# Two queues for the small exchanges of a spectral layer, another order of its partitions, and contiguous writes in one copy

## The chip, the cores and the metric

The kernel runs on one core of one Trainium2 chip. The metric is the device time of one execution in microseconds (us).

Names: PE is TensorE, ACT is ScalarE, DVE is VectorE, POOL is GpSimd, SP is SyncE. SPq is SyncE's own queue of instructions, PEld are PE's weight loads.

## The reference

Two layers, each a global spectral filter (2-D FFT of the normalised activations, a product with complex weights, inverse FFT) and a channel MLP, both with residuals. x is 2048 x 576 in bf16.

```python
def spectral(x, w_r, w_i):
    X = jnp.fft.rfft2(x.astype(jnp.float32), axes=(-2, -1)) * (w_r + 1j * w_i)
    return jnp.fft.irfft2(X, s=x.shape[-2:], axes=(-2, -1)).astype(jnp.bfloat16)
# mlp: gelu(layernorm(y) @ w1 + b1) @ w2 + b2 with 4608 hidden columns
for _ in range(2):
    x = x + spectral(layernorm(x), w_r, w_i)
    x = x + mlp(layernorm(x))
```

## The kernel before

The FFT over the 2048 rows is cut into 16 x 128. Between its two factors the data must change partitions, which no matmul here does: that is an *exchange*. Each of 16 tiles (128 partitions x 580 values of bf16, 145 KB) is written by one DMA into 8 partitions of a big array. A layer has two: exchange 1 brings y1 into v_sb, between the first DFT stage and the second (`dft_u`); exchange 2 brings h into b_sb, before the last inverse DFT (`idft_v`). Each consumer needs a slice of all tiles, so it starts when the last exchange has landed. PE meanwhile multiplies zeros (`keep_busy`).

```python
    # first stage, one tile: DFT over the columns, scaled by the layernorm's 1/std while it is copied out of PSUM
            z = work.tile([P, 2, KP], BF16, tag="z", bufs=3)
            nc.scalar.activation(
                out=z[:].rearrange("p r (j o) -> p r o j", o=2),     # writes every second element
                in_=pz[:, :, 0:KP].rearrange("p o (r j) -> p r o j", r=2),
                func=ACT.Copy, scale=self.st.pop(("rs", t)),
            )
    # ... dft_v makes y1 from z; then
            exchange(self.vx, t, y1)

    def exchange(dst, slot, src):
        p0 = 32 * (slot // 4) + slot % 4
        ins = nc.sync.dma_start(out=dst[p0 : p0 + 29 : 4], in_=src).ins   # 128 partitions -> 8
        # ... (declares that exchanges into other partitions don't wait for each other)

    # second stage
        keep_busy(12)                       # zeros while exchange 1 lands
        # dft_u, weigh, join, idft_c -> h, exchange(hx, E_ORDER[n], h)
    # last inverse stage
            for n in self.early[:2]:
                self.put_x(n)               # work that needs no exchange
            keep_busy(16)                   # zeros while exchange 2 lands
            self.idft_v(0)                  # first reader of exchange 2
```

Weights for the middle stage are loaded during the first stage by DMAs that GpSimd issues, paced by marks on earlier instructions. GpSimd issues in program order, so an issue that waits holds up those behind it.

## Time and profile before

747.18 us, the median of 6 runs (746.68 to 747.85); the profiled run has a span of 745.1 us.

| quantity of layer 0, us from the start of the span | before |
|---|---|
| first matmul that makes a y1 | 10.98 |
| last y1 copy ends | 37.80 |
| first matmul on v_sb (exchange 1 is in) | 41.63 |
| last h copy ends | 64.93 |
| first matmul on b_sb (exchange 2 is in) | 69.99 |

The first part of the page: each engine's busy time, its share of the span and its instructions.

```profile
PE 726.9 (98%) x5038; PEld 454.1 (61%) x5038; DVE 273.0 (37%) x932; ACT 314.3 (42%) x530; POOL 61.6 (8%) x114
```

PE at 98% does not mean that nothing can be won: the fillers count as busy. The view of waits says where PE still stood idle in the first 75 us. The columns are: who waited, on what, for how long in total, how often, the longest.

```profile
PE pss_156 L337 <- DVE xf L315: 2.0, 1, 2.0
PE psb_705 L496 <- DMA v_sb<-shared_113: 1.3, 1, 1.3
PE pss_1036 L567 <- DMA b_sb<-shared_691: 0.9, 1, 0.9
```

The second and third lines are what the change is after. The timeline around exchange 1 (start, duration, engine, line, operation; in brackets the idle time before it and what ended it):

```profile
37.09 0.40 ACT L399 CAST shared_113<-pss_680 128x290 bf16<-128x290 f32 x1 [0.94 <-PE pss_680 L398]
37.34 0.46 DVE L399 CAST shared_113<-pss_684 128x290 bf16<-128x290 f32 x1
37.54 2.77 PE L214 MATMUL pss_692<-zeros 128*128 128x512 bf16 x12 [0.24 <-ACT shared_113 L399]
38.17 0.61 SPq L481 DMA_DIRECT2D v_sb<-shared_113  x1
41.63 0.66 PE L496 MATMUL psb_705<-v_sb,c_f_83 128*128 128x290 bf16 x4 [1.32 <-DMA v_sb<-shared_113]
...
```

The last y1 is complete at 37.34 + 0.46 = 37.80. Its DMA is issued at 38.17, its data land at 41.39 (read from the semaphore's updates in the trace), and the reader starts at 41.63. These three pieces, 0.37 + 3.22 + 0.24 us, are the gap of 3.83 us. Layer 1's gap is 2.98. The same around exchange 2:

```profile
64.47 0.46 DVE L531 CAST shared_691<-psb_997 128x290 bf16<-128x290 f32 x1 [1.11 <-PE psb_997 L527]
...
64.49 0.67 PE L593 MATMUL psb_1009<-x_sb,halves 128*128 128x288 bf16 x4
...
65.48 3.65 PE L214 MATMUL pss_1019<-zeros 128*128 128x512 bf16 x16
...
69.99 0.60 PE L567 MATMUL pss_1036<-c_r_84,b_sb 128*128 128x256 bf16 x4 [0.87 <-DMA b_sb<-shared_691]
```

And one z copy of the first stage, in which ACT is busy nearly all the time; a plain copy of the same size takes 0.65 us.

```profile
23.65 0.94 ACT L423 ACTIVATE z<-psb_445,rs 128x580 bf16<-128x580 f32 x1
```

Busy times by stretches of 2 us, of PE, PEld, DVE, ACT and POOL, then the granted clock, the mean busy share of the 16 DMA engines and what they moved in GB/s (which is KB/us). The exchanges alone keep the share near one half:

```profile
14.00:16.00 2.00, 1.68 (x16) 1.03 (x13) 1.66 (x5) 2.00 (x5) 0.84 (x2) 1.00 0.85 208
...
32.00:34.00 2.00, 2.00 (x21) 1.59 (x19) 1.90 (x8) 1.72 (x5) 0.00 (x0) 1.00 0.57 191
34.00:36.00 2.00, 1.87 (x22) 1.53 (x21) 1.34 (x2) 1.54 (x3) 0.00 (x0) 1.00 0.53 178
```

### The profile page before, as it was taken

To read this page: it belongs to the slowest core of one execution; us is meant where nothing else is said; L and a number is where in the kernel's file an instruction comes from. 1 tells how busy PE (TensorE), PEld (TensorE's weight loads), DVE (VectorE), ACT (ScalarE), POOL (GpSimd) and SP (SyncE) were. 2 spreads that over 40 slices of the span, in tenths; PEclk is the share of its full clock that TensorE was granted. 3 is DMA by queue.
4 is the path that set the end of the run, shared out by engine and by line. 5 is a ranking of instruction groups with operands and counts; after the bars stand their busy time and mean duration, and the time that the engine had idled before them with its cause. 6 is when DMAs were issued, how large, how long until landed. Compare 5 with 4: busy or idle time off the path is not lost. (4 is left out here: it accounts for less than half of the span.)

```text
span 745.1 us, 12420 instructions
## 1 busy us (share of the span) xinstructions
PE 726.9 (98%) x5038; PEld 454.1 (61%) x5038; DVE 273.0 (37%) x932; ACT 314.3 (42%) x530; POOL 61.6 (8%) x114
## 2 busy tenths in 40 slices
PE   7989999999999999999999999999999999999998
PEld 4655744784488447844775575467547744774476
DVE  7975860366036603630364869001400140010011
ACT  7865865015521552155324777530362045105600
POOL 4120012001000100000004000020100010000000
PEclk9999999999999999999999999999999999999999
DMA  8744825311121112110028401460001010200000
GB/s 272 232 139 162 250 88 189 100 44 34 29 62 52 35 27 63 44 35 0 22 40 235 122 10 59 149 158 18 36 10 44 17 44 0 45 17 8 1 17 17
DMA packets 49417, 54.45 MB, mean 73 GB/s; under 512 B 29892, under 2 KB 41104, under 8 KB 49360
## 3 DMA queue, kind: packets, MB, share of 16 engines
q1 hardware_dynamic: 41328, 23.99, 12.5%
q0 software_dynamic: 7600, 29.10, 12.2%
q8 instruction: 39, 0.64, 0.3%
q10 hardware_dynamic: 432, 0.58, 0.2%
q14 instruction: 18, 0.15, 0.1%
HBM read 29.34 MB, written 8.59 MB: 51 GB/s over the span
## 5 line engine op out<-in xcount | busy, mean ns | idle before, releaser
L806 PEld LDWEIGHTS <-h_sb 128*128 128x128 bf16 x2304 | 224.9, 98 | 58.6 <-issue 1.0
L761 PEld LDWEIGHTS <-w_sb 128*128 128x128 bf16 x1152 | 109.4, 98 | 142.4 <-issue 17.2
L274 DVE BATCH_NORM_STATS2 stats<-x_sb 128x6 f32<-128x288 bf16 x110 | 43.8, 440 | 1.1 <-DMA x_sb<-in_A_x_dram 1.1
L720 DVE TENSOR_SCALAR xn<-x_sb,mv,rs 128x576 bf16<-128x576 bf16 x24 | 9.4, 426 | 66.7 <-DMA quad_1769<-xn 27.7
L769 PEld LDWEIGHTS <-w1r_sb 64*128 64x128 bf16 x288 | 10.8, 94 | 24.5 <-issue 17.0
L802 DVE TENSOR_TENSOR xb<-x_sb,b_bc 128x576 f32<-128x576 bf16 x32 | 23.9, 748 | 0.0
L723 POOL COPY xn<-xn 128x64 bf16<-128x64 bf16 x24 | 6.4, 267 | 155.2 <-DVE xn L720 155.2
L527 PEld LDWEIGHTS <-h_sb 128*128 128x128 bf16 x128 | 12.1, 97 | 11.6 <-issue 6.2
L496 PEld LDWEIGHTS <-c_f_83 128*128 128x128 bf16 x128 | 12.3, 97 | 8.8 <-issue 3.2
L775 ACT ACTIVATE h_sb<-psb_5993,b_sb 128x512 bf16<-128x512 f32 x2 | 1.3, 684 | 37.9 <-PE psb_5993 L769 37.9
L775 ACT ACTIVATE h_sb<-psb_7189,b_sb 128x512 bf16<-128x512 f32 x2 | 1.3, 684 | 37.8 <-PE psb_7189 L769 37.8
L775 ACT ACTIVATE h_sb<-psb_6591,b_sb 128x512 bf16<-128x512 f32 x2 | 1.3, 683 | 37.8 <-PE psb_6591 L769 37.8
L829 DVE TENSOR_TENSOR x_sb<-psb_7429,xb 128x576 bf16<-128x576 f32 x1 | 0.8, 757 | 43.4 <-PE psb_7429 L806 43.4
L829 DVE TENSOR_TENSOR x_sb<-psb_4049,xb 128x576 bf16<-128x576 f32 x1 | 0.8, 758 | 39.5 <-PE psb_4049 L806 39.5
L214 PEld LDWEIGHTS <-zeros 128*128 128x128 bf16 x95 | 9.4, 100 | 9.5 <-issue 1.7
L352 DVE TENSOR_TENSOR xf<-ef 128x256 bf16<-128x256 f32 (+1 forms) x56 | 13.6, 305 | 0.5
L829 DVE TENSOR_TENSOR x_sb<-psb_6233,xb 128x576 bf16<-128x576 f32 x1 | 0.8, 757 | 33.6 <-PE psb_6233 L806 33.6
L829 DVE TENSOR_TENSOR x_sb<-psb_6831,xb 128x576 bf16<-128x576 f32 x1 | 0.8, 758 | 33.6 <-PE psb_6831 L806 33.6
L435 PEld LDWEIGHTS <-c_k_82 128*128 128x128 bf16 x120 | 11.1, 98 | 2.4
L419 PEld LDWEIGHTS <-xT 128*128 128x128 bf16 x96 | 9.6, 101 | 3.9 <-issue 1.1
L829 DVE TENSOR_TENSOR x_sb<-psb_3245,xb 128x576 bf16<-128x576 f32 x1 | 0.8, 757 | 28.7 <-PE psb_3245 L806 28.7
L678 ACT ACTIVATE h_sb<-x_sb 128x576 bf16<-128x576 bf16 x16 | 11.2, 699 | 0.1
(1367 smaller groups left out, 1500.6 us busy)
## 6 DMA issues: line engine op xcount, KB each, us to landing
w_sb<-in_B_w_dram SPq DMA_DIRECT2D x16, 288.0 KB
v_sb<-in_B_w_dram POOLq DMA_DIRECT2D x4, 1152.0 KB, 5.9
h_sb<-const_i POOLq DMA_DIRECT2D x8, 384.0 KB, 6.6
shared_1465<-in_B_w_dram POOLq DMA_DIRECT2D x2, 1440.0 KB, 7.9
shared_5390<-in_B_w_dram POOLq DMA_DIRECT2D x2, 1440.0 KB, 7.5
v_sb<-shared_113 SPq DMA_DIRECT2D x16, 145.0 KB
b_sb<-shared_691 SPq DMA_DIRECT2D x16, 145.0 KB
v_sb<-shared_4645 SPq DMA_DIRECT2D x16, 145.0 KB
```

The source lines that it names most:

```text
L214: nc.tensor.matmul(pw[:], lhsT=zeros[:], rhs=zeros[:, 0:1].to_broadcast([P, 512]), start=True, stop=True)
L274: nc.vector.bn_stats(out=stats[:, h, :], in_=x_sb[:, t, h * DH : (h + 1) * DH])
L352: nc.vector.tensor_tensor(out=xf[:, at0 : at0 + 2 * n].rearrange("p (g d) -> p g d", g=2), in0=ef[:, :, first : first + n], in1=ef[:, :, b ...
L419: nc.tensor.matmul(pz[:, o, 0:KP], lhsT=xT[:, ci, :], rhs=c_fd[:, 3 * o + q, :], start=(q == 0), stop=(q == 2),)
L435: nc.tensor.matmul(py[:, r, 0:KP], lhsT=c_k1[:, pl, :], rhs=z[:, ri], start=(q == 0), stop=(q == 1))
L496: nc.tensor.matmul(px[:, o, 0:KP], lhsT=c_f2[:, e, pl, :], rhs=vx[:, e, ri, :], start=(q == 0), stop=(q == 1))
L527: nc.tensor.matmul((ph, odd)[o][:, o, 0:KP], lhsT=i1[:, n % 4, pl, :], rhs=xp[:, ri, :], start=(q == 0), stop=(q == 1))
L678: nc.scalar.activation(out=at(h_sb, [P, D], 512 * 34), in_=x_sb[:, self.quad[i], :], func=(ACT.Copy, ACT.Square)[k], accum_out=self.s12[:, ...
L761: nc.tensor.matmul(acc[p][q], lhsT=w1_sb[:, ci, fc * 128 : (fc + 1) * 128], rhs=yT[:, ci, :], start=(first and ci == 0), stop=(not first a ...
L769: nc.tensor.matmul(acc[p][q], lhsT=w1r_sb[rows, p, :], rhs=yT[rows, 4, :], start=first, stop=not first)
L802: nc.vector.tensor_tensor(out=xb[:], in0=xr, in1=b2_bc[:].rearrange("p (h n) -> p h n", h=2), op=ALU.add)
L806: nc.tensor.matmul(po[:, h, 0:DH], lhsT=hts[fc][:, i * 128 : (i + 1) * 128], rhs=w2_chunk(fc)[:, h * DH : (h + 1) * DH], start=(fc == 0), ...
```

## The change

The intent: (a) let ACT write z contiguously and read PSUM in steps instead; (b) spread layer 0's exchanges over two queues, so that they use more than eight DMA engines; (c) let successive tiles write to partitions of different halves.

```diff
-SLOT_ROWS = [8 * (4 * (p // 32) + p % 4) + (p // 4) % 8 for p in range(128)]
+SLOT_ROWS = [8 * (4 * (0, 2, 1, 3)[p // 32] + p % 4) + (p // 4) % 8 for p in range(128)]
@@ dft_d
-                out=z[:].rearrange("p r (j o) -> p r o j", o=2),
-                in_=pz[:, :, 0:KP].rearrange("p o (r j) -> p r o j", r=2),
+                out=z[:].rearrange("p r (j o) -> p r j o", o=2),
+                in_=pz[:, :, 0:KP].rearrange("p o (r j) -> p r j o", r=2),
@@ dft_v                      (room is None in layer 1)
-            exchange(self.vx, t, y1)
+            exchange(self.vx, t, y1, nc.gpsimd if self.room is not None and order.index(t) % 2 == 0 else nc.sync)
@@
-    def exchange(dst, slot, src):
-        p0 = 32 * (slot // 4) + slot % 4
-        ins = nc.sync.dma_start(out=dst[p0 : p0 + 29 : 4], in_=src).ins
+    def exchange(dst, slot, src, queue=nc.sync):
+        p0 = 64 * (slot // 4 % 2) + 32 * (slot // 8) + slot % 4
+        if queue is nc.gpsimd:
+            nc.gpsimd.nop()
+        ins = queue.dma_start(out=dst[p0 : p0 + 29 : 4], in_=src).ins
@@ idft_c                     (queues is 2 in layer 0, 1 in layer 1)
-            exchange(hx, E_ORDER[n], h)
+            exchange(hx, E_ORDER[n], h, nc.gpsimd if queues == 2 and n % 2 == 0 and n < NT - 2 else nc.sync)
```

Below, "tile 14" and "tile 15" are the last two in order of work.

More of the change, by code (lines that the diff above doesn't have):

```diff
@@ L485, in exchange, with middle @@
         before.append(ins)
-    def middle(vx, hx, wks, i1s, loads):
+    def middle(vx, hx, wks, i1s, loads, queues):
         st = {}
@@ L912 @@
             }
-        middle(vx, hx, wks, i1s, mid_loads)
+        middle(vx, hx, wks, i1s, mid_loads, 2 - li)
         if li == 0:
```

## The prediction

> **What bounds the kernel.** TensorE is busy 98% of 745.1 us (page, first part), mostly in the two MLPs, which the change leaves alone. But part of that is filler: matmuls on zeros while PE waits for exchanges. The change acts on the spectral stages of layer 0, the first 70 us. There (timeline) three things can give:
>
> 1. *Exchange 1.* The last y1 copy ends at 37.80 us, the filler at 40.31; the first matmul on v_sb starts at 41.63. The waits view gives PE 1.3 us for DMA v_sb<-shared. This gap is 3.83 us; layer 1's is 2.98.
> 2. *Exchange 2.* Last h copy 64.93; filler ends 69.13; first matmul 69.99: PE waits 0.9 us for b_sb. Layer 1 waits nothing here.
> 3. *The z copies.* From 10 to 36 us ScalarE is busy 93-100%, VectorE 84-99% (stretches of 2 us); a pair of tiles takes 3.60 or 3.84 us.
>
> **Why the exchanges are late.** From 30 to 41 us and 59 to 67 us only SyncE's queue moves data, at a DMA share flat at 0.53-0.54 and 175-180 KB/us: half of the 16 engines. The Trainium skill ("DMA: Bandwidth & Descriptors", on why a DMA increments its semaphore by 16) says that the engine count is the largest up to 16 dividing both slowest dimensions, here 128 and 8, and that SyncE takes the lowest; the trace agrees. Until 30 us weight loads share these engines and the exchange gets only about 35 KB/us, so a backlog builds: at 38.2 us (last issue) 2.6 exchanges are still to move. An exchange alone (layer 1) takes 1.3 us to its first packet and 1.2 us of packets.
>
> **What changes.** Half of layer 0's exchanges (8 of 16; 7 of 16 in the second) go to GpSimd. The same section says that its 8-engine copies go round by a cursor, so about half of these should land on the idle upper eight: engines 0-7 lose a quarter of 290 KB each, 3.3 us at 22 KB/us. No backlog should remain at the last issue. Added: GpSimd issues of 0.55-0.75 us each, on an engine 8% busy, in line with the loads, which have slack. I expect the first v_sb matmul 2.8 us after the last y1 (gain 1.0) and the first b_sb matmul right behind the filler (gain 0.8). The filler caps these at 1.3 and 0.9.
>
> **z** takes 0.92 us for 580 elements, a plain copy 0.65; at 290, 0.59 against 0.40. So about 0.11 us is fixed ("ScalarE: Activation LUTs", What ACT_TABLE_LOAD costs: 93 ns for a pointer operand) and 0.28 ns per element is the strided write. Contiguous writes save up to 0.16 us each, if reading PSUM alternately from two banks is free, which nothing in the trace shows. VectorE takes about 3.55 us a pair and then binds, so 14 copies save 0.8 us of stage, not 2.2. In layer 1 these copies hide under PE.
>
> **Sum:** 747.2 - 1.0 - 0.8 - 0.8 = 744.6 us; range 742.9 to 746.9. Faster by over 2%: 0.01; within 2%: 0.98; slower by over 2%: 0.01.
>
> **What would show it.** z mean about 0.77 us; last y1 near 37.0; DMA share above 0.54 within 30-38 us; gap from y1 to the first v_sb matmul about 2.8 us; no PE wait for b_sb in layer 0; layer 1 unchanged.
>
> **What would make it wrong.** The alternate PSUM read may cost more than the write saves: with z at 1.1 us ScalarE binds and the stage grows by 2 us, giving about 747. GpSimd's copies may all use the lower eight engines, or land late behind loads in the same rings; then the exchange gains vanish. Waits for exchanges in GpSimd's order might hold loads up.

## More of the kernel before

All runs told here were with a granted clock of 0.995 to 1.0.

In exchange 1, tile 14 goes to GpSimd and tile 15 to SyncE.

The filter's weights are tiny (0.05 x 0.02 in standard deviation): the comparison with the reference tolerates much in the spectral path.

## The result, and the profile after

The changed kernel takes 746.57 us, the median of 10 runs (745.92 to 747.90), against 747.49 us for the kernel before in the same rounds (746.51 to 749.60, 20 runs). The ratio is 0.9989, with a 95% interval from 0.9980 to 0.9998; a ratio here is the mean time of one kernel's fast runs over that of the other's of the same rounds, so it isn't quite the ratio of the medians. That is 0.1 to 1.5 us gained.

The page of after:

```profile
PE 727.3 (98%) x5038; PEld 454.8 (61%) x5038; DVE 273.1 (37%) x932; ACT 310.1 (42%) x530; POOL 71.3 (10%) x129
```

ACT has 4.2 us less to do, POOL 9.7 us more and 15 instructions more. PE's waits in the first 75 us:

```profile
PE pss_156 L337 <- DVE xf L315: 2.3, 1, 2.3
PE psb_713 L498 <- DMA v_sb<-shared_113: 1.5, 1, 1.5
...
PE psb_1024 L595 <- DVE shared_699 L533: 0.4, 1, 0.4
```

The wait for v_sb grew a little, the one for b_sb is gone, and a new one of 0.4 us has come, in front of `put_x`. Around exchange 1:

```profile
37.73 0.45 DVE L399 CAST shared_113<-pss_692 128x290 bf16<-128x290 f32 x1
37.80 2.77 PE L214 MATMUL pss_700<-zeros 128*128 128x512 bf16 x12 [0.24 <-ACT shared_113 L399]
...
38.12 0.60 POOL L483 DMA_DIRECT2D v_sb<-shared_113  x1 [2.19 <-DVE shared_113 L442]
38.25 0.61 SPq L483 DMA_DIRECT2D v_sb<-shared_113  x1
42.11 0.66 PE L498 MATMUL psb_713<-v_sb,c_f_83 128*128 128x290 bf16 x4 [1.53 <-DMA v_sb<-shared_113]
```

Tile 15's issue now follows its y1 at once (0.06 us), as tile 14 no longer occupies SyncE before it. But its data need 3.62 us from issue to landing (41.87), and the gap is 0.06 + 3.62 + 0.24 = 3.92 us. Around exchange 2:

```profile
64.95 0.46 DVE L533 CAST shared_699<-psb_1012 128x290 bf16<-128x290 f32 x1 [1.11 <-PE psb_1012 L529]
...
65.47 0.65 PE L595 MATMUL psb_1024<-x_sb,halves 128*128 128x288 bf16 x4 [0.43 <-DVE shared_699 L533]
...
66.44 3.65 PE L214 MATMUL pss_1034<-zeros 128*128 128x512 bf16 x16
69.93 0.60 PE L569 MATMUL pss_1051<-c_r_84,b_sb 128*128 128x256 bf16 x4
```

`idft_v` has no bracket now: it follows the filler. A z copy and the DMA stretches:

```profile
24.46 0.77 ACT L423 ACTIVATE z<-psb_449,rs 128x580 bf16<-128x580 f32 x1
```

```profile
14.00:16.00 2.00, 1.96 (x19) 1.44 (x17) 0.78 (x4) 2.00 (x5) 1.96 (x3) 1.00 0.27 65
...
32.00:34.00 2.00, 2.00 (x22) 1.65 (x21) 1.92 (x8) 1.70 (x4) 0.60 (x1) 1.00 0.77 205
34.00:36.00 2.00, 2.00 (x21) 1.58 (x20) 1.48 (x4) 1.26 (x4) 0.60 (x1) 1.00 0.70 192
```

The engines' share rose by a third from 32 to 36 us, what they moved by 7 to 8%. At 14 us, on the other hand, the DMAs ran nearly dry: GpSimd's queue stood waiting for the first y1, issued that exchange at 14.04, and only then the loads behind it.

Put together, each step measured within its own profile so that a later start doesn't enter:

| us | before | after | difference | predicted |
|---|---|---|---|---|
| first y1 matmul to last y1 copy | 26.82 | 25.93 | -0.89 | -0.8 |
| last y1 to first v_sb matmul | 3.83 | 3.92 | +0.09 | -1.0 |
| first v_sb matmul to last h | 23.30 | 23.30 | 0.00 | 0 |
| last h to first b_sb matmul | 5.06 | 4.52 | -0.54 | -0.8 |
| sum (before: 10.98 to 69.99; after: 12.25 to 69.93) | 59.01 | 57.68 | -1.33 | -2.6 |

The sum of -1.33 us lies inside the timed interval. The two spans nevertheless are equal (745.1 and 745.2 us), because the profiled run of after started its first y1 matmul 1.27 us later, ahead of anything that the change touches. That start is a lottery: over these two profiles and those of the ten experiments that leave the start alone, it lies anywhere between 10.98 and 12.41 us.

### The profile page after: what moved, and what is told of

Same layout as the page of the kernel before. It is cut to its first block, busy times and chain, and to the rows that moved or that the text cites. A ratio compares the mean times of both kernels' runs of the same rounds, so it can differ in the third digit from the quotient of the medians.

```text
span 745.2 us, 12420 instructions
## 1 busy us (share of the span) xinstructions
PE 727.3 (98%) x5038; PEld 454.8 (61%) x5038; DVE 273.1 (37%) x932; ACT 310.1 (42%) x530; POOL 71.3 (10%) x129
```

## The experiments

Each kernel's edit is shown against the changed kernel, unless another is named. Every kernel below was called correct by the comparison. "Issue to landing" is that of the last exchange, tile 15's.

### What each part does: z_only, no_z, ex1_sync, ex1_late

*z_only* is the kernel before with the contiguous z writes alone; the exchanges, all on SyncE, and the partitions are those of before. Its edit, against the kernel before:

```diff
-                out=z[:].rearrange("p r (j o) -> p r o j", o=2),
-                in_=pz[:, :, 0:KP].rearrange("p o (r j) -> p r o j", r=2),
+                out=z[:].rearrange("p r (j o) -> p r j o", o=2),
+                in_=pz[:, :, 0:KP].rearrange("p o (r j) -> p r j o", r=2),
```

> Kernel before plus the contiguous z writes alone. Stretch from the first y matmul to the last y1 copy: 26.8 us before, 25.9 us in the changed kernel. Theory T (exchange 1 is a train of copies on 8 engines, 0.80 us apart, whose end the loads set, not the computation): stretch falls to about 25.9, but the gap from the last y1 copy to the first v_sb matmul grows from 3.8 to about 4.6, so the total gains at most 0.3 us. Rival (the gap is a fixed latency after the last y1): gap stays 3.8 and the total falls by 0.9 us to 0.9988 of before. Exchange 2 keeps its PE wait of 0.9 us under both.

*no_z* is the changed kernel with the old z copy.

```diff
-                out=z[:].rearrange("p r (j o) -> p r j o", o=2),
-                in_=pz[:, :, 0:KP].rearrange("p o (r j) -> p r j o", r=2),
+                out=z[:].rearrange("p r (j o) -> p r o j", o=2),
+                in_=pz[:, :, 0:KP].rearrange("p o (r j) -> p r o j", r=2),
```

> The changed kernel with the strided z writes of before: queues and ports alone. z 0.92 us, stretch about 26.8 us. Theory T: the train ends about when it does in the changed kernel, so with y1 0.9 us later the gap is about 3.1 to 3.3 us (3.9 changed, 3.8 before) and exchange 2 gains its 0.5 us: total about 1.0 to 1.2 us below before (0.9985). Rival (the queues gain nothing in exchange 1, z gains 0.9 by itself): gap 3.8 to 3.9, total 0.4 us below before.

*ex1_sync* sends the whole first exchange through SyncE.

```diff
-            exchange(self.vx, t, y1, nc.gpsimd if ... else nc.sync)
+            exchange(self.vx, t, y1, nc.sync)
```

> The changed kernel with all of exchange 1 on SyncE; exchange 2 still alternates. Theory T (waits for y1 in GpSimd's order hold the weight loads up): the last weight load of the first stage lands near 32 us as before, not near 36; the gap is about 4.6 us, as in z_only, since all 16 copies are one train again; exchange 2 has no PE wait. Total about 0.6 us below before. Rival (GpSimd's own latency sets the gap of the changed kernel, loads do not matter): gap falls to about 3.0 us, total 2 us below before.

*ex1_late* uses GpSimd only for the even tiles from 8 on, after the weight loads have been issued.

```diff
-  ... order.index(t) % 2 == 0 else nc.sync)
+  ... order.index(t) % 2 == 0 and order.index(t) >= 8 else nc.sync)
```

> The changed kernel, but in exchange 1 only tiles 8, 10, 12 and 14 of the order go to GpSimd, behind all weight loads in its order. Theory T: the loads are issued as in the kernel before (last one lands near 32 us), the two queues then share the rest, and the gap falls to about 3.0 to 3.3 us; total about 1.7 to 2.0 us below before. Rival (a GpSimd exchange is slow in itself, or shares the lower eight engines): gap stays 3.8 to 4.2 us, total 0.9 us below before or less.

| kernel | y1 stretch | y1 to issue | issue to landing | gap 1 | gap 2 | last load lands | us, median (ratio, 95% interval) |
|---|---|---|---|---|---|---|---|
| before | 26.82 | 0.37 | 3.22 | 3.83 | 5.06 | 31.99 | |
| after | 25.93 | 0.06 | 3.62 | 3.92 | 4.52 | 36.17 | 746.57 (0.9989, 0.9980 to 0.9998) |
| z_only | 25.94 | 0.39 | 3.64 | 4.27 | 4.64 | 31.81 | 746.98 (0.9991, 0.9977 to 1.0005) |
| no_z | 26.62 | 0.07 | 3.57 | 3.87 | 4.52 | 35.10 | 748.12 (1.0001, 0.9985 to 1.0017) |
| ex1_sync | 25.94 | 0.38 | 3.48 | 4.10 | 4.52 | 32.78 | 747.95 (1.0000, 0.9984 to 1.0015) |
| ex1_late | 26.20 | 0.06 | 3.59 | 4.33 | 4.66 | 33.26 | 747.88 (0.9999, 0.9985 to 1.0013) |

These four shared one chip, on which the kernel before took 748.04 us (746.91 to 750.25). The timed rounds separate none of them; the stages do.

In this table the stretch is 25.93 or 25.94 us with the new z copy except in ex1_late, and 26.6 to 26.8 without it. In ex1_late PE's slow start (explained under warm_trim) reached into the stretch: the first four y1 matmuls took 0.92 us, against 0.66 in the others. The z part is right as predicted, and the alternate reads from PSUM cost nothing that shows. But the stages aren't independent: z_only gains 0.88 us in the stretch and loses 0.44 of it again in gap 1 (4.27 against 3.83). For the same reason the effect of the queues on gap 1 depends on what it is compared with: after is 0.09 us longer than before, but 0.35 shorter than z_only and 0.18 shorter than ex1_sync, which have the new z copies too. Each is a single profile.

For gap 1 the theory of the prediction (a train of exchanges whose backlog the loads set) failed in ex1_late. The loads land 2.9 us earlier than in after, and the gap is longer, not 3.0 to 3.3 as expected. 0.67 us of that gap lie between the landing and the first matmul, where the others have 0.24. The trace tells why: PE's sequencer goes through its waits for the exchanges in pairs of semaphores, 0.106 us apart, and in ex1_late the last exchange stands in the first of six pairs, in after in the third of four. So four more steps follow the landing, 0.42 us; without them the gap would be about 3.9 (an estimate from these numbers). Issue to landing itself, 3.59 us, hadn't moved. Holding up the loads is therefore real (the last one is issued at 25.99 instead of 22.55 us) but isn't what eats the gain.

Gap 2 deserves care: z_only has all of exchange 2 on SyncE, as before has, and yet reads 4.64 us where before reads 5.06. Two profiles of the old arrangement differ by 0.42 us, so the new one's gain is between 0.1 and 0.5 us.

### Is there a backlog at all: few_sync, few_after, no14

*few_sync* has the first exchange on SyncE and moves two weight loads of the first stage (384 KB each by the page) into the middle stage; *few_after* does only the latter.

```diff
-    for n, (kind, j) in enumerate(first[:-3]):
+    for n, (kind, j) in enumerate(first[:-5]):
...
-                0: [lambda b: load_w(3, 0, b)],
-                1: [lambda b: load_w(3, 1, b)],
+                0: [lambda b: load_f2(3, b), lambda b: load_w(3, 0, b)],
+                1: [lambda b: load_i1(2, b), lambda b: load_w(3, 1, b)],
```

> All first exchanges on SyncE again, as in ex1_sync, and two of the stage's last weight loads (393 KB each) moved behind it into the middle stage. Theory T (the end of exchange 1 is the end of a train on eight engines, whose backlog the weight loads set): with the last load of the stage landing near 28 us instead of 32.8, the train has 4 us more to catch up (0.8 us each, one new exchange every 1.8 us), so no backlog is left at the last issue; the gap from the last y1 copy to the first v_sb matmul falls from 4.10 (ex1_sync) to about 3.0, layer 1's value. Rival F (the end has a fixed latency of 3.2 to 3.6 us after the last issue whatever came before): gap stays near 4.0. Time under T 1 us below ex1_sync's, under F equal.

> The changed kernel (first exchanges alternate) with the same two loads moved behind the stage. Theory T: gap from 3.92 to about 3.0, as the backlog is gone. Rival S (the exchange of tile 14, on GpSimd, slows the last one on SyncE, which runs beside it): the last exchange still lands 3.2 or more after its issue, gap about 3.7, longer than few_sync's.

*no14* is the changed kernel with tile 14 on SyncE.

```diff
-  ... order.index(t) % 2 == 0 else nc.sync)
+  ... order.index(t) % 2 == 0 and order.index(t) < NT - 2 else nc.sync)
```

> The changed kernel, but the exchange of the last even tile (14) goes to SyncE; the other seven even ones stay on GpSimd, as in exchange 2. Rival S: without GpSimd's copy beside it the last exchange lands sooner, gap about 3.4 instead of 3.92. Theory T: the last two then queue behind each other and whatever backlog the held-up loads left on the lower engines, so the gap stays at 3.9 to 4.2.

| kernel | y1 to issue | issue to landing | landing to matmul | gap 1 | last load lands | middle stage | us, median (ratio, 95% interval) |
|---|---|---|---|---|---|---|---|
| few_sync | 0.39 | 3.26 | 0.25 | 3.89 | 28.86 | 24.61 | 748.10 (1.0000, 0.9985 to 1.0016) |
| few_after | 0.06 | 3.70 | 0.24 | 4.01 | 31.14 | 24.86 | 748.26 (1.0001, 0.9987 to 1.0015) |
| no14 | 0.39 | 3.42 | 0.14 | 3.95 | 35.44 | 23.30 | 747.43 (0.9996, 0.9980 to 1.0012) |

(The kernel before took 748.38 us beside these, 746.86 to 749.32.)

few_sync answers the question. Its train is gone: the last exchanges, issued 0.7 to 2.3 us apart from 31.64 us on, land 2.85, 2.83, 2.78, 3.14, 3.15, 3.00 and 3.27 us after their issue. Yet the gap is 3.89 us: 0.2 us shorter than in ex1_sync (4.10), the same kernel with the loads in place, 0.4 shorter than in z_only (4.27), and no shorter than in the kernel before (3.83). **At most a few tenths of backlog were there to win back at the end, not 1.0 us.** That 2.6 exchanges are on the way when the last is issued is simply what a latency of 2.8 us looks like when they come every 0.7 to 1.3 us. few_sync's y1 stretch, 27.14 us, is longer than the others' 25.9 because PE's slow start reached into it (the first four y1 matmuls took 1.17 us and the next six 1.66, against 0.66 and 0.91 in ex1_sync); the pieces of its gap aren't touched by that.

Moving the loads also cost 1.3 to 1.6 us of the middle stage in these two. few_after's trace reads: the first exchange 2 of GpSimd, issued behind five more loads at 48.71, lands 9.1 us later; h has a ring of eight buffers, and PE waits 1.2 us on one copy into it ("ACT shared L537"). This reading wasn't tested, and the price isn't fixed: of the three kernels of the next section, which have the same loads moved, few_ports, with the old partitions, pays nothing (23.30 us) and has no such wait. Whether part (c) of the change causes the difference wasn't tested; it is one profile each.

no14 fell between its expectations: the last exchange lands 3.42 instead of 3.62 us after its issue, but it is issued 0.33 us later, behind tile 14's. The two queue arrangements cost the same to 0.03 us.

### What lengthens the last exchange: early14, flip, few_ports

All three start from few_after, whose DMAs are quiet at the end. *early14* takes the neighbour away: it sends tile 14's slot already at tile 10, with tile 10's data. Its output is wrong, which doesn't matter for the time. (The comparison didn't notice; with filter weights of about 0.001 one wrong tile of sixteen in one layer is below its tolerance.)

```diff
-            exchange(self.vx, t, y1, nc.gpsimd if ... else nc.sync)
+            if self.room is None or order.index(t) != 14:
+                exchange(self.vx, t, y1, nc.gpsimd if ... else nc.sync)
+            if self.room is not None and order.index(t) == 10:
+                exchange(self.vx, order[14], y1, nc.gpsimd)
```

> Wrong result on purpose. few_after (no backlog at the end), but tile 14's part of v_sb is sent already at tile 10, from tile 10's data, so that the last exchange, on SyncE, has nothing beside it. Rival S (two exchanges in the same microsecond share a limit that is not the number of engines, about 200 KB/us): the last one takes 2.8 us from issue to landing, as layer 1's lone ones do, instead of 3.70, and the gap from last y1 to first v_sb matmul is 0.06 + 2.8 + 0.24 = 3.1 instead of 4.01. Rival F (fixed 3.2 to 3.6 us in layer 0): 3.5 or more of gap.

*flip* adds one small copy of the same form on GpSimd at tile 0, to turn by eight engines the cursor that says where GpSimd's next copy begins.

```diff
+            if self.room is not None and order.index(t) == 0:
+                nc.gpsimd.dma_start(out=at(b_sb, [P, 16, 2, KP])[0:29:4, :, 0, 0:64], in_=y1[:, 0, 0:64])
```

> few_after with one more small GpSimd copy of eight partitions at tile 0, into an array that is free at that time. If GpSimd's copies go round the engines by a cursor, tile 14's then runs on the other half of the engines than in few_after, where its records lie beside SyncE's with 13 of 16 engines busy (0.81 from 39.0 to 39.5 us). Expected: the DMA share at the end no longer exceeds 0.55. If sixteen engines were worth their number, sharing eight makes the last landing later: 4.0 to 4.3 us after the issue. Rival S (a limit of about 200 KB/us whatever the number of engines): it stays within 0.2 of 3.70.

*few_ports* has the partitions of before.

```diff
-SLOT_ROWS = [8 * (4 * (0, 2, 1, 3)[p // 32] + p % 4) + ...
+SLOT_ROWS = [8 * (4 * (p // 32) + p % 4) + ...
-        p0 = 64 * (slot // 4 % 2) + 32 * (slot // 8) + slot % 4
+        p0 = 32 * (slot // 4) + slot % 4
```

> few_after with the partitions of before, so that tiles 14 and 15 both write into partitions 64 to 127 instead of one into each half. If writing into both halves helps, the last landing moves from 3.70 us after its issue to 4.0 or later and the shared rate falls; if the limit is on the reading side, where every exchange reads all 128 partitions, it stays within 0.15 of 3.70.

| kernel | y1 to issue | issue to landing | gap 1 | tile 14's issue to landing | middle stage |
|---|---|---|---|---|---|
| few_after | 0.06 | 3.70 | 4.01 | 3.15 | 24.86 |
| early14 | 0.07 | **2.79** | **3.10** | (sent early) | 24.76 |
| flip | 0.06 | 3.64 | 3.94 | 2.80 | 23.97 |
| few_ports | 0.07 | 3.54 | 3.84 | 3.10 | 23.30 |

These three were run for the profile, with one timed round: 747.73, 748.36 and 748.28 us (two runs each), beside 748.07 us of the kernel before, which separates nothing.

Timeline of few_after around the exchange (POOL is tile 14's issue, SPq tile 15's):

```profile
37.14 0.60 POOL L483 DMA_DIRECT2D v_sb<-shared  x1 [2.19 <-DVE shared L442]
37.27 0.61 SPq L483 DMA_DIRECT2D v_sb<-shared  x1
...
41.22 2.02 PE L498 MATMUL psb<-v_sb,c_f 128*128 128x290 bf16 x15 [1.61 <-DMA v_sb<-shared]
```

The same of early14:

```profile
37.68 0.61 SPq L486 DMA_DIRECT2D v_sb<-shared  x1
40.71 2.52 PE L501 MATMUL psb<-v_sb,c_f 128*128 128x290 bf16 x19 [0.70 <-DMA v_sb<-shared]
```

With nothing beside it the last exchange needs 2.79 us, what a lone one needs in layer 1 of the kernel before (2.81), and PE's wait falls from 1.61 to 0.70 us. So the neighbour costs 0.9 us, about what the change had been expected to save. The other profiles bear this out: the last exchange needs 3.54 to 4.05 us in the eight kernels where GpSimd's exchange of tile 14 is issued 0.13 to 0.15 us before it, and 3.22 to 3.64 in the five where tile 14's comes 0.7 us before it on SyncE's own queue. A neighbour costs on either queue. Now the DMA stretches at that time, of few_after, flip and early14 (last two columns: busy share of 16 engines, GB/s):

```profile
38.50:39.00 0.50, 0.50 (x4) 0.20 (x2) 0.00 (x0) 0.00 (x0) 0.00 (x0) 1.00 0.49 72
39.00:39.50 0.50, 0.50 (x3) 0.10 (x1) 0.00 (x0) 0.00 (x0) 0.00 (x0) 1.00 0.81 193
...
```

```profile
38.50:39.00 0.50, 0.50 (x4) 0.20 (x3) 0.00 (x0) 0.00 (x0) 0.00 (x0) 1.00 0.53 75
39.00:39.50 0.50, 0.50 (x5) 0.20 (x2) 0.00 (x0) 0.00 (x0) 0.00 (x0) 1.00 0.46 177
...
```

```profile
39.00:39.50 0.50, 0.50 (x4) 0.26 (x3) 0.00 (x0) 0.00 (x0) 0.00 (x0) 1.00 0.43 70
39.50:40.00 0.50, 0.50 (x3) 0.01 (x1) 0.00 (x0) 0.00 (x0) 0.00 (x0) 1.00 0.52 186
...
```

In few_after 13 of 16 engines (0.81) moved 193 KB/us; in flip, where the cursor has put both exchanges on the same eight, 7 to 8 engines (0.46) moved 177; a lone exchange at its best reaches 186. And the last landing is the same in both, 3.70 and 3.64 us. **The second eight engines were indeed used, as predicted, and brought nothing.** The packets show it directly. This is the mean number of busy engines and the mean time of the packets (SyncE's have 1160 B, GpSimd's 4640 B) that start in each quarter of a microsecond, worked out from few_after's trace:

```
 from    GpSimd's queue          SyncE's queue
38.75    8.1 busy, 179 ns        1.2 busy, 161 ns
39.00    8.2 busy, 179 ns        5.0 busy, 159 ns
39.25    7.3 busy, 179 ns        6.9 busy, 211 ns
39.50    4.2 busy, 179 ns        7.1 busy, 140 ns
39.75    0.8 busy,  -            8.5 busy,  53 ns
40.00    0                       8.6 busy,  52 ns
```

While GpSimd's exchange runs, SyncE's packets take about three to four times their 52 ns, although they are on other engines; when it ends they are at full speed. (Not all of this is the neighbour: early14's lone exchange also begins slowly, with 79, 140 and 95 ns in its first three quarters. But it has sent 80 packets after four quarters, few_after's only 32.) What the two exchanges share isn't shown. It isn't the engines (flip). It isn't one half of the partitions on the writing side either: few_ports, where both write into partitions 64 to 127, lands 0.16 us sooner, not later. The expectation had 0.15 as its bound for "the limit is on the reading side", where every exchange reads all 128 partitions; that fits, but no run varied the reading side, so it stays open. It isn't a general limit of about 200 KB/us: weight loads with exchanges moved 284 to 308 KB/us in the kernel before between 16 and 22 us.

### A faster version: warm_trim, and an attempt to better it

*warm_trim* leaves the exchanges alone and changes two fillers.

```diff
-                    keep_busy((5, 1, 1, 1)[i])
+                    keep_busy((6, 8, 1, 1)[i])
...
-            keep_busy(16)
+            keep_busy(14)
```

> Two pieces that don't touch the exchanges. (1) Filler before the first tiles: 6 and 8 matmuls on zeros in place of 5 and 1, which fill the idle PE from 4.7 to 7 us. If the late full clock of PE causes the spread at the start, the first matmul of dft_v moves from 12.25 us to about 11 us (10.98 in the profile of before) and the spread between runs (744.1 to 746.1 us spans) narrows to its lower part: about 0.5 to 0.8 us off the median. If the x tiles' arrival causes it, it stays near 12. (2) The filler before exchange 2's first reader has 14 matmuls instead of 16: if the filler is what that reader now waits for, the gap after the last h goes from 4.52 to about 4.07; if the exchange is, it stays at 4.5 with a wait for b_sb. Both right: 1.0 to 1.2 us below the changed kernel, near 745.4 us.

*best* adds one moved load to it.

```diff
-    for n, (kind, j) in enumerate(first[:-3]):
+    for n, (kind, j) in enumerate([f for f in first[:-3] if f != ("i1", 2)]):
...
-                2: [lambda b: load_i1(3, b)],
+                2: [lambda b: load_i1(2, b), lambda b: load_i1(3, b)],
```

> A candidate that beats both: warm_trim with one weight load of the first stage (393 KB) moved into the middle stage, where few_after moved two and lost 1.5 us by it. Expected: the last load of the stage lands near 33 us instead of 35.3, the gap from y1 to v_sb falls from 4.35 to about 4.1, the middle stage stays at 23.3, and the time is 0.2 to 0.3 us below warm_trim's 745.42, near 745.2. If the middle stage grows it is slower than warm_trim.

| kernel | first y1 matmul | gap 1 | middle | gap 2 | us, median (all runs) | before beside it | ratio, 95% interval |
|---|---|---|---|---|---|---|---|
| after | 12.25 | 3.92 | 23.30 | 4.52 | 746.57 (745.92 to 747.90) | 747.49 | 0.9989, 0.9980 to 0.9998 |
| warm_trim | 10.40 | 4.35 | 23.31 | 4.08 | 745.42 (745.15 to 746.21) | 748.38 | 0.9968, 0.9955 to 0.9980 |
| best | 10.16 | 3.85 | 24.45 | 4.31 | 745.79 (745.40 to 746.18) | 748.07 | 0.9968, 0.9955 to 0.9982 |

The start of after on PE:

```profile
1.00 2.31 PE L214 MATMUL pss_122<-zeros 128*128 128x512 bf16 x5 [1.00 <-DVE h_sb L230]
...
7.01 0.72 PE L337 MATMUL pss_156<-ident,xf 128*128 128x128 bf16 x5 [2.30 <-DVE xf L315]
7.52 1.66 PE L419 MATMUL psb_167<-c_fd,xT 128*128 128x290 bf16 x6
...
9.93 1.66 PE L419 MATMUL psb_199<-c_fd,xT 128*128 128x290 bf16 x6
```

And of warm_trim:

```profile
1.00 2.74 PE L214 MATMUL pss<-zeros 128*128 128x512 bf16 x6 [1.00 <-DVE h_sb L230]
...
4.06 3.01 PE L214 MATMUL pss<-zeros 128*128 128x512 bf16 x8
7.13 0.44 PE L337 MATMUL pss<-ident,xf 128*128 128x128 bf16 x5
7.40 0.91 PE L419 MATMUL psb<-c_fd,xT 128*128 128x290 bf16 x6
...
9.04 0.91 PE L419 MATMUL psb<-c_fd,xT 128*128 128x290 bf16 x6
```

The same six matmuls take 1.66 us in after and 0.91 in warm_trim. In the profile of before, the second six (at 9.71 us) already took 0.91, in after they didn't: this is the start's lottery. The Trainium skill says where it comes from ("TensorE: Matmul & The Clock Gate", Part 1: The HAM clock gate): PE runs at half clock until it has been busy for a window of about 3.4 us, and these windows run freely, without regard to when the kernel starts. The trace agrees: a sixth matmul of 512 columns adds 2.74 - 2.31 = 0.43 us at the start, while sixteen take 3.65 later, about 0.23 each. With the idle time from 4.7 to 7.0 us filled, the clock is up at the first real work, the first y1 matmul moves from 12.25 to 10.40 us, and the runs' spread shrinks from 2.0 us (10 runs) to 1.1 (5 runs). Nothing but zeros was added, so zeros count as work here.

The shorter filler took 0.44 us from gap 2, as expected: `idft_v` had waited for the filler and not for the exchange, which lands at 67.82, just 0.26 us before its first reader at 68.08. Part of the gain was lost again in gap 1 (4.35 us), since the stage starts earlier while its last load still lands at 35.28: here a backlog does count, and the last exchange takes 4.05 us to land. In best, moving one load brings gap 1 to 3.85 but lengthens the middle stage by 1.14 us, and the time isn't better: warm_trim and best have the same ratio, 2.4 us below the kernel before (0.0032 x 748). (few_ports, with the old partitions, moved two loads at no cost to that stage; this wasn't tried together with warm_trim.) Against after both ran in other rounds, so the difference, about 1.2 us by warm_trim's median and 1.6 by the ratios, wasn't timed side by side.

## Why the prediction was right or wrong

The range (742.9 to 746.9 us) held; the point, 744.6, was 2.0 us too low. That the range held is partly luck: the result lies 0.3 us below its upper end, with about a third of the expected gain (0.9 of 2.6 us by the medians), and the largest term of the sum didn't come at all. In turn:

- **z: right.** Predicted 0.77 us a copy and 0.8 us of stage; measured 0.74 to 0.77 and 0.89 (z_only 0.88). The one doubt, that alternating PSUM reads might cost, was unfounded. But the sum took this gain as independent of the gap behind it, and in z_only half of it was lost there.
- **Exchange 1: the term that failed.** "No backlog should remain at the last issue [...] I expect the first v_sb matmul 2.8 us after the last y1 (gain 1.0)." Measured: a loss of 0.09 against before (a gain of 0.35 against z_only). Two steps of the argument fell. First, the train's backlog was only a small part of what lengthened the gap: few_sync has none and keeps 3.89 us, 0.2 less than ex1_sync. The comparison with layer 1 (2.98) misled, because there the last exchange comes alone, 3.3 us after the one before it, whereas here two come within 0.7 us. Second, "the idle upper eight" were used (a share of 0.81, and flip for the contrary) but two exchanges side by side moved 193 KB/us where eight engines alone move 177 to 186. What would have been won by the free queue, 0.31 us of issue, the slower landing took back (3.22 to 3.62). Only without a neighbour (early14) does the gap come to 3.10 us, near the 2.8 predicted.
- **Exchange 2: right in direction, smaller in size.** PE's wait for b_sb (0.9 us) vanished, as predicted, but the gap shrank by 0.54 and not 0.8. Its lower bound is the filler, which now begins later: `put_x` used to start 0.44 us ahead of the last h copy's end and now starts 0.06 us after it, as it waits for that copy (0.4 us in the waits). The prediction took the filler as fixed. With z_only's 4.64 us for the old arrangement, the true gain may be as small as 0.1 us.
- **The warnings.** "Waits for exchanges in GpSimd's order might hold loads up" came true (last load issued 25.99, not 22.55, and landed 36.17, not 31.99), and so did "land late behind loads": from 17 to 29 us GpSimd's exchanges took 8 to 10 us. Neither decided the gap, as ex1_late shows: with the loads back near their old times its last exchange still took 3.59 us. "May all use the lower eight engines" didn't come true.
- **What wasn't foreseen:** the start's spread of 1.4 us, larger than the change, which makes single profiles of two kernels look equal when the stages differ by 1.3 us. The line that pointed at it, PE's wait of 2.0 us at 4.8 us, was in the profile of before.

The same skill page that the prediction used has a section that it should have used as well ("DMA: Bandwidth & Descriptors", Issuing engines are not separate DMA queues): transfers started from several engines run on the same DMA engines and interleave, and issuing from several saves only "the time on the sequencer it takes to initiate the DMA". Here that time was about 0.3 us, and the runs agree with the sentence even where the engines were different ones.

## What to carry to other kernels

A wait for a transfer is a sum of issue, latency, packets and neighbours: compare it with the same transfer alone, and with one that has the same arrivals, before calling the surplus a backlog. A higher busy share of DMA engines is not more bytes; read the GB/s beside it. And read stages within one profile, from their own start: look first whether the start itself varies, since filling PE's early idle time was worth more here than the whole change.

## What the Trainium skill lacked or had wrong

- "DMA: Bandwidth & Descriptors", on how many engines a DMA takes: the number is confirmed (SyncE's exchanges alone keep the share at 0.53, 8 of 16, and each is announced by eight landings), and GpSimd's cursor (one small extra copy moved the share at the end from 0.81 to 0.46). That SyncE takes the lowest eight can't be read from these traces, whose packets carry no engine number; the prediction's "the trace agrees" holds for the number alone. Lacking: what two such copies do to each other. Two copies of 128 rows into 8 partitions on disjoint sets of eight engines moved 193 KB/us together, against 177 to 186 for eight engines, and packets of 1160 B took 140 to 211 ns instead of 52 (79 to 140 at the start of a lone one).
- The same page, Latency and other measured facts, gives a first byte after about 0.6 us from SyncE and 1 us from GpSimd. Counted from the end of the issue (0.6 us long on both) the first packet of data came after 0.63 us on SyncE (early14) and 0.65 us on GpSimd (few_after): no difference here. From start of issue to landing, 145 KB took 2.79 us alone on SyncE and 2.80 to 3.15 beside a neighbour on GpSimd (flip, few_after).
- "TensorE: Matmul & The Clock Gate", Part 1: confirmed (0.43 and 0.23 us for 512 columns). Lacking, beyond its general caveat on the clock gate's trace events: that the profile's granted clock reads 1.00 all through the slow start, so that only the matmuls' durations show it (six of 290 columns: 1.66 against 0.91 us).
- "ScalarE: Activation LUTs", What ACT_TABLE_LOAD costs, gives 186 ns, 93 ns for a pointer operand and 0.833 ns per element, an estimate of 762 ns for the contiguous z copy; 744 to 771 were measured. Lacking on that page: the price of writing every second element of bf16, 0.91 to 0.95 us for the same copy ("SBUF — State Buffer" speaks of strides, but gives no such time), and that reading two PSUM banks by turns cost nothing here.
